# A planner that lands loads in the order of their issue, one load moved behind another, and a new table of due times

## The chip, the cores and the metric

The kernel runs on one core of one Trainium2 chip. The metric is the device time of one execution in microseconds, smaller being better. The time before is a median over three executions. The profile is of one further execution, with its own time.

## The reference: what is computed

Two layers, one after the other. The first is a linear attention with polynomial sketches; B = 4 batches, H = 4 heads, S = 1088 tokens, D = 32, r = 8:

```python
def phi(x):                       # x: (b, h, s, d)
    a = np.einsum('rd,bhsd->bhsr', S1, x)
    b = np.einsum('rd,bhsd->bhsr', S2, x)
    return np.einsum('bhsi,bhsj->bhsij', a, b).reshape(*x.shape[:-1], r * r)
q_p, k_p = (phi(q), phi(k))
kv = np.einsum('bhsf,bhsd->bhfd', k_p, v)
z = np.sum(k_p, axis=2)
num = np.einsum('bhsf,bhfd->bhsd', q_p, kv)
den = np.einsum('bhsf,bhf->bhs', q_p, z)[..., None] + 1e-06
attn = num / den
```

The second is a gated feed-forward layer over the 4352 tokens (B * S) with 128 channels (H * D) and 1536 hidden units: `np.maximum(x @ w_gate, 0) * (x @ w_val) @ w_out`. Inputs and output are float32.

## The kernel before

**Layout and stages.** A batch is 1088 tokens, held as 128 partitions by 34 chunks. For each batch a class K makes the keys' side: two transposes on DVE (kt1, L531), sketches on PE (ksk, L542), transposes back (kt2, L555), the sum z (L570, L584 and the small DVE steps zc and wc), the products of the two sketches on POOL (kphi, L599), the cast of v to 16 bits in two halves (vc, L606, on ACT for batches 1 to 3), the product kv on PE (L613) and its eviction by DVE into bz (kve, L620). A class Q makes the queries' sketches and the denominator (qt1 L1034, qsk L719 or L735, qt2 L741, bw L769, dn L776, rd L781, an L801). A class G makes the query product (qphi, L867), turns it (through PE at L885 and ACT at L892 for the first three groups, through a transposing DMA at L875 for the later ones), multiplies it with bz (num, L901) and writes x, the feed-forward's input, in 16 bits (L908 or L913).

**Feed-forward.** A class F does one unit: gate matmuls g (L960), relu by ACT (L965), value matmuls v (L972), their product h by DVE (L982), and the output matmuls o (L994), which accumulate over the units of a group. In every sixth unit from the fourth on ACT copies the value (vcp, L977) and POOL makes the product instead (hp, L987). There are 103 units: 0 to 23 on batch 0, 24 to 47 on batch 1 and so on, the last seven on the tokens that are left of all batches. At a group's end ACT evicts (L1002) and SP stores (L1011, L1016).

**What sets the order of the work.** Nothing is scheduled at run time. A class Plan holds all operations with an engine, an estimated duration, predecessors, PSUM banks to take and drop, and a due time. `Plan.run` (L89) simulates the engines and starts one operation after the other: it takes the one that can start first (L118), and then, among the operations of the same engine that can start within a short look-ahead, the one with the earliest due time (L120). The order of the starts is the order in which instructions are put into each engine's queue, and each queue is worked off in order. Due times come from the consumers' due times (`dues`, L82), and at the end a hand-held table `shift` (L1107) adds to single operations' due times, in microseconds: negative is earlier.

**Loads.** SP issues all of them on one queue. Up to q1 they stand in program order with fixed times of landing in the plan (`LAND`, L405). The loads after these, v1, k2, q2, v2, k3, q3 and v3, are operations (`load`, L438): one on SP for issuing, one on a further serial engine of the plan, "DMA", for the transfer. Loads of v are four DMAs each (L216), those of k and q one (L210, L273). Buffers of later batches first serve as staging for the feed-forward's weights (L250): k of batch 2 holds two thirds of w_out, v of batch 1 the last third. So k2's load waits for the casts wo0 and wo1, and v1's load for the cast wo2 (POOL, L428); these are the predecessors at L444 and L445. Where two issued transfers stand at the plan's "DMA" engine at once, L120 takes the one that is due earlier, whatever the order of issue.

Of the kernel before, what the change touches and what calls it, by code (L numbers as in the profile page):

```python
# [35 lines left out]
class Plan:  # L36
# [52 lines left out]
    def run(self):  # L89
        todo = [o for o in self.ops if o.start is None]  # L90
        need = {o: sum(a.start is None for a in o.after) for o in todo}
        ready = [o for o in todo if not need[o]]
        n = 0
        while ready:
            for o in ready:
                o.at = max([self.free[o.eng]] + [
                    a.start + a.busy if a.eng == o.eng == "PE" else a.done for a in o.after])
            now = min(o.at for o in ready)

            left = dict(self.banks)  # L100
            wants = sorted((o for o in ready if any(l.banks is None for l in o.take)),
                           key=lambda o: (o.due, o.seq))
            for o in wants:
                near, o.pick, rest = o.at <= now + self.HOLD, [], dict(left)
                for l in o.take:
                    if l.banks is None:
                        got = self.choose(rest, l.n, o.at)
                        if got is None:
                            o.at = None
                            break  # L110
                        o.at = max([o.at] + [rest.pop(b) for b in got])
                        o.pick.append((l, got))
                if near and o.at is not None:
                    left = rest
            can = [o for o in ready if o.at is not None]
            if not can:
                raise RuntimeError("no bank for any of " + ", ".join(o.name for o in ready))
            o = min(can, key=lambda o: (o.at, o.due, o.seq))  # L118

            o = min((c for c in can if c.eng == o.eng and c.at <= o.at + self.look(o)),  # L120
                    key=lambda c: (c.due, c.seq))
            o.start = o.at
            o.done = o.start + o.vis
            self.free[o.eng] = o.start + o.busy
            for l in o.take:
                if l.banks is None:
                    l.banks = next(got for m, got in o.pick if m is l)
                    for b in l.banks:
                        del self.banks[b]
            for l in o.drop:  # L130
                l.left -= 1
                l.free_at = max(l.free_at or 0.0, o.done)
                if not l.left:
                    for b in l.banks:
                        self.banks[b] = l.free_at
            ready.remove(o)
            for s in o.succ:
                need[s] -= 1
                if not need[s]:
                    ready.append(s)  # L140
            n += 1
        assert n == len(todo), [o.name for o in todo if o.start is None]
        return max(o.done for o in todo)
# [3 lines left out]
def kernel(  # L147
# [12 lines left out]
    nc = tc.nc  # L160
# [45 lines left out]
    def flat(src, b):  # L206
        return src[b].rearrange("h (p c) d -> (h p) (c d)", c=NC)

    def load_k(eng, b):
        eng.dma_start(out=k_sb[b][:, 0:NC * D], in_=flat(k, b))  # L210
# [38 lines left out]
    v1, v2 = (v32[b].rearrange("p h c -> p (h c)") for b in (1, 2))  # L249
# [22 lines left out]
    def load_q(eng, b):  # L272
        eng.dma_start(out=q_sb[b], in_=flat(q, b))  # L273

    def load_vs(b):
        for a in (0, 2, 1, 3):
            load_v(nc.sync, b, a)
# [143 lines left out]
    wcast = {}  # L421
# [14 lines left out]
    issue = {}  # L436

    def load(name, fn, after):  # L438
        n = 4 if name[0] == "v" else 1
        issue[name] = i = P.add("SP", f"{name} issue", 0.44 * n, fn, after,  # L440
                                rec=1.95 - 0.44 * n)
        land[name] = P.add("DMA", name, 2.7 if n == 4 else 1.4, None, [i], rec=0.15)

    load("v1", lambda: load_vs(1), [wcast["wo2"]])  # L444
    load("k2", lambda: load_k(nc.sync, 2), [wcast["wo0"], wcast["wo1"]])  # L445
    load("q2", lambda: load_q(nc.sync, 2), [])
    load("v2", lambda: load_vs(2), [wcast["wg2"], wcast["wv2"], land["v1"]])
    load("k3", lambda: load_k(nc.sync, 3), [wcast["wg0"], wcast["wv0"]])
# [587 lines left out]
    qt1 = {}  # L1036
# [64 lines left out]
    for o in P.ops:  # L1101
# [3 lines left out]


    shift = {  # L1107
# [16 lines left out]
    }  # L1124
    for o in P.ops:
        o.due += shift.get(o.name, 0.0)
# [46 lines left out]
```

## Time and profile before

| | |
|---|---|
| median of 3 executions | 100.71 us (99.73 to 101.25) |
| the profiled execution's own time | 101.48 us |
| its span, first to last instruction | 99.70 us |
| granted TensorE clock | 1.00 of full speed |
| busy in the span | PE 93.9, DVE 83.1, ACT 81.0, POOL 61.2 us |
| first feed-forward matmul | 13.77 us |
| DMA | 13.28 MB, mean 133 GB/s |

Rows of the profile name an engine, a line of the kernel, the operation, and the tiles as out<-in. PE is TensorE's matmuls, PEld its weight loads, SPq the issuing of DMAs on SP. A row of the timeline starts with the start and the duration in us, consecutive instructions of one kind merged; in square brackets stands idle time of the engine just before and what ended it.

### The profile page before, as it was taken

To read this page: it belongs to the slowest core of one execution; us is meant where nothing else is said; L and a number is where in the kernel's file an instruction comes from. 1 tells how busy PE (TensorE), PEld (TensorE's weight loads), DVE (VectorE), ACT (ScalarE), POOL (GpSimd) and SP (SyncE) were. 2 spreads that over 40 slices of the span, in tenths; PEclk is the share of its full clock that TensorE was granted. 3 is DMA by queue.
4 is the path that set the end of the run, shared out by engine and by line. 5 is a ranking of instruction groups with operands and counts; after the bars stand their busy time and mean duration, and the time that the engine had idled before them with its cause. 6 is when DMAs were issued, how large, how long until landed. Compare 5 with 4: busy or idle time off the path is not lost.

```text
span 99.7 us, 3026 instructions
## 1 busy us (share of the span) xinstructions
PE 93.9 (94%) x1129; PEld 61.7 (62%) x1129; DVE 83.1 (83%) x181; ACT 81.0 (81%) x160; POOL 61.2 (61%) x66
## 2 busy tenths in 40 slices
PE   6999999999799999999999999999999999999950
PEld 2265678677466665666756765657666565668920
DVE  5979959989799999999999699876869777696940
ACT  3411899978699988989998489899899989999920
POOL 6148569699959699669969944799422404224000
PEclk9999999999999999999999999999999999999999
DMA  2999999786620678950435004015352300210122
GB/s 50 323 250 268 406 410 414 246 274 172 187 78 2 143 136 283 325 151 7 105 85 132 0 7 109 0 29 97 92 117 50 105 7 0 73 33 0 28 57 80
DMA packets 16783, 13.28 MB, mean 133 GB/s; under 512 B 8064, under 2 KB 14464, under 8 KB 16768
## 3 DMA queue, kind: packets, MB, share of 16 engines
q1 hardware_dynamic: 16736, 13.08, 45.3%
q8 instruction: 9, 0.15, 0.7%
q14 instruction: 6, 0.05, 0.2%
q10 hardware_dynamic: 32, 0.00, 0.0%
HBM read 9.14 MB, written 2.23 MB: 114 GB/s over the span
## 4 chain that ended last, share of the span: by engine, by line
PE 67%; DVE 9%; DMA 7%; POOL 5%; SPq 4%; issue 3%; ACT 2%; DVEq 0%; ACTq 0%
PE ps L994 21%; PE ps L960 20%; PE ps L972 19%; DMA q_sb<-in_q_dram 4%; DMA v<-in_v_dram 3%; POOL qqp L867 3%; PE ps L901 3%; SPq L216 3%; PE ps L613 2%; PE ps L735 2%; PE ps L542 1%; ACT g_sb L965 1%; DVE qT L1034 1%; DVE ht L982 1%; POOL wo L428 1%
## 5 line engine op out<-in xcount | busy, mean ns | idle before, releaser
L982 DVE TENSOR_TENSOR ht<-g_sb,ps 128x512 f16<-128x512 f16 (+1 forms) x87 | 55.4, 672 | 10.1 <-ACT g_sb L965 5.2
L965 ACT ACTIVATE g_sb<-ps 128x512 f16<-128x512 f32 (+1 forms) x103 | 56.2, 605 | 5.0 <-PE ps L960 3.7
L960 PE MATMUL ps<-xT,wg 128*128 128x512 f16 (+1 forms) x120 | 37.1, 348 | 0.6 <-ACT g_sb L965 0.6
L972 PE MATMUL ps<-xT,wv 128*128 128x512 f16 (+1 forms) x120 | 37.2, 347 | 0.0
L994 PEld LDWEIGHTS <-ht 128*128 128x128 f16 x408 | 27.6, 98 | 13.5 <-POOL ht L987 3.3
L994 PE MATMUL ps<-wo,ht 128*128 128x128 f16 x408 | 34.7, 219 | 0.2
L987 POOL TENSOR_TENSOR ht<-g_sb,v_sb 128x512 f16<-128x512 f16 x16 | 18.7, 1168 | 18.2 <-ACT g_sb L965 13.5
L599 POOL TENSOR_TENSOR kp<-kab 128x512 f16<-128x512 f32 (+1 forms) x15 | 17.0, 1159 | 2.1 <-DVE kab L555 2.0
L960 PEld LDWEIGHTS <-wg 128*128 128x128 f16 x120 | 13.1, 115 | 5.1 <-issue 1.8
L867 POOL TENSOR_TENSOR qqp<-qan,qabc 128x1024 f16<-128x1024 f32 (+1 forms) x9 | 15.7, 1759 | 0.6 <-DVE qan L801 0.4
L972 PEld LDWEIGHTS <-wv 128*128 128x128 f16 x120 | 12.9, 114 | 4.3 <-issue 0.9
L977 ACT COPY v_sb<-ps 128x512 f32<-128x512 f32 x16 | 9.6, 601 | 0.0
L330 PE MATMUL ps<-zero 128*128 128x512 f16 (+6 forms) x23 | 6.7, 409 | 1.0 <-DVE maskkv L295 1.0
L606 ACT CAST v<-v 128x576 f16<-128x576 f32 x7 | 4.7, 681 | 2.4 <-DMA v<-in_v_dram 2.4
L1002 ACT ACTIVATE o_sb<-ps 128x512 f32<-128x512 f32 (+1 forms) x10 | 5.4, 544 | 1.3 <-PE ps L994 1.2
L1034 DVE STREAM_TRANSPOSE qT<-q_sb 128x576 f32<-128x576 f32 (+4 forms) x10 | 6.1, 614 | 0.5 <-DMA q_sb<-in_q_dram 0.5
L913 ACT CAST xT<-ps 128x512 f16<-128x512 f32 (+1 forms) x9 | 5.0, 554 | 0.7 <-PE ps L901 0.7
L531 DVE STREAM_TRANSPOSE kT<-k_sb 128x544 f32<-128x544 f32 (+2 forms) x8 | 5.5, 719 | 0.0
L901 PE MATMUL ps<-qpt,bz 128*128 128x512 f16 (+2 forms) x26 | 5.3, 305 | 0.0
L741 DVE STREAM_TRANSPOSE qabc<-ps 128x512 f32<-128x512 f32 (+2 forms) x8 | 5.3, 692 | 0.0
L330 PEld LDWEIGHTS <-zero 128*128 128x128 f16 x23 | 2.4, 120 | 3.1 <-issue 1.4
L613 PEld LDWEIGHTS <-kp 128*128 128x128 f16 (+1 forms) x72 | 3.5, 98 | 1.3 <-issue 0.2
(85 smaller groups left out, 64.3 us busy)
## 6 DMA issues: line engine op xcount, KB each, us to landing
v<-in_v_dram SPq DMA_DIRECT2D x15, 144.0 KB, 5.7
out_dram<-o_sb SPq DMA_DIRECT2D x28, 64.0 KB, 1.8
k_sb<-in_k_dram SPq DMA_DIRECT2D x3, 544.0 KB, 5.2
q_sb<-in_q_dram SPq DMA_DIRECT2D x3, 544.0 KB, 7.5
k_sb<-in_moe_w_out_dram SPq DMA_DIRECT2D x2, 256.0 KB, 5.2
q_sb<-in_q_dram SPq DMA_DIRECT2D x1, 416.0 KB, 5.6
k_sb<-in_k_dram SPq DMA_DIRECT2D x1, 288.0 KB, 2.8
k_sb<-in_k_dram SPq DMA_DIRECT2D x1, 256.0 KB, 3.0
```

Of the source, the lines that this page charges most:

```text
L330: nc.tensor.matmul(PS[:, W_BANK, 0:m * w], zero, zero[:, None, 0:w].to_broadcast([128, m, w]), start=True, stop=True)
L599: eng.tensor_tensor(out=self.kp[:, lo:hi].rearrange("p x g (i a c) -> p (x g i) a c", i=2, a=R), in0=src[:, 0, :, :, None].to_broadcast([1 ...
L867: eng.tensor_tensor(out=self.qp[:, lo:hi].rearrange("p x g (i a c) -> p (x g i) a c", i=2, a=R), in0=a_in[:, :, :, None].to_broadcast([128 ...
L901: nc.tensor.matmul(o[:, 0:n * 128].rearrange("f (x t) -> f x t", x=n)[:, :, t], self.ks[b or 0].bz[:, p], self.pt[:, 0:n, p, t], start=(p ...
L960: nc.tensor.matmul(bank(self.lg)[:, y * W:(y + 1) * W], wblock(wg, j), x, start=True, stop=True, skip_group_check=True)
L965: nc.scalar.activation(out=self.gs[:, 0:self.cols], in_=bank(self.lg)[:, 0:self.cols], func=ACTF.Relu)
L972: nc.tensor.matmul(bank(self.lv)[:, y * W:(y + 1) * W], wblock(wv, j), x, start=True, stop=True, skip_group_check=True)
L977: nc.scalar.copy(out=self.vs, in_=bank(self.lv))
L982: nc.vector.tensor_tensor(out=self.ht[:, 0:w], in0=self.gs[:, 0:w], in1=bank(self.lv)[:, 0:w], op=ALU.mult)
L987: nc.gpsimd.tensor_tensor(out=self.ht, in0=self.gs, in1=self.vs, op=ALU.mult)
L994: nc.tensor.matmul(o[:, s], self.ht[:, y * W + s * 128:y * W + (s + 1) * 128], wo[:, j // 4, (j % 4) * DM:(j % 4 + 1) * DM], start=(j == 0 ...
L1034: nc.vector.transpose(qT[b][:, lo * 32:hi * 32], q_sb[b][:, lo * 32:hi * 32])
```

## The change

In `Plan.run` a transfer is chosen by the time its issue started instead of by its due time. The issue of k2 gets v1's issue as a further predecessor, so that it comes after it on SP. The table of shifts is replaced: 74 entries before, 116 after, 47 names in both. The entries on units (g, v, h, o) go from 54 to 89 and reach unit 76 instead of 52. The core of the diff:

```diff
             o = min((c for c in can if c.eng == o.eng and c.at <= o.at + self.look(o)),
-                    key=lambda c: (c.due, c.seq))
+                    key=lambda c: (c.after[-1].start if c.eng == "DMA" else c.due, c.seq))
...
     load("v1", lambda: load_vs(1), [wcast["wo2"]])
-    load("k2", lambda: load_k(nc.sync, 2), [wcast["wo0"], wcast["wo1"]])
+    load("k2", lambda: load_k(nc.sync, 2), [wcast["wo0"], wcast["wo1"], issue["v1"]])
...
     shift = {
...
-        "h 33": -8.2, "h 38": 2.8, "kphi 1 6": -2.9, "ksk 3 0": 0.7,
-        "kt1 3 1": 2.5, "kv 0 4 1": 1.8, "kv 1 0 0": -0.7, "kv 2 0 0": 3.3,
-        "kve 1": 1.1, "num 1,0": 1.7, "num 1,4": 0.8, "o 14": 9.8,
...
-        "qaT 0,0": 5.9, "qsk 2,0": -1.1, "qt1 1 0": 0.2, "qt1 2 16": 4.8,
...
-        "vc 1 0": -1.7, "vc 1 1": -0.2, "w 2": -0.5, "z 3": -2.2,
+        "g 10": -0.4, "g 12": -2.5, "g 16": 0.9, "g 18": 0.4, "g 19": 1.3,
...
+        "h 14": -6.9, "h 24": 0.8, "kphi 2 0": 8.0, "kphi 2 4": 4.9,
+        "ksk 0 1": 4.1, "ksk 3 0": 0.7, "kt1 3 0": -4.6, "kt1 3 1": 2.1,
+        "kv 0 8 0": 2.0, "kv 1 6 0": 1.3, "kv 2 0 0": 3.9, "kve 1": 3.1,
+        "num 1,0": 1.7, "num 1,4": 1.6, "num 2,4": -2.2, "num 3,0": 0.9,
...
+        "o 70": 1.9, "o 8": 5.1, "qphi 0,0 0": 5.1, "qsk 0,0 0": 5.6,
+        "qt1 3 0": -1.6, "qt1 3 16": -1.0, "qt2 2,0 1": 2.3, "qt2 3,0 0": 5.4,
+        "rd 3,0": -0.6, "sx": -2.9, "v 0": -1.5, "v 11": -0.5, "v 12": -1.1,
...
+        "z 2": -0.2, "zc 0": -3.2,
     }
```

27 rows, old and new, of the table shift are left out of this document.

## The prediction

> **What bounds the kernel now.** I read the page first, then the PE groups kept apart by shape, the busy time by stages, and last the order of work on SP, ACT, POOL, DVE and PE around the one stage that is not full. The page's busy times, with their share of the span:
>
> ```profile
> PE 93.9 (94%) x1129; PEld 61.7 (62%) x1129; DVE 83.1 (83%) x181; ACT 81.0 (81%) x160; POOL 61.2 (61%) x66
> ```
>
> A busy PE need not be PE at its peak, so I take the spacing of its matmuls from the chain of waits (start, us, what) and the counts from the groups by shape (count | busy, mean ns):
>
> ```profile
> 43.88 0.89 PE ps L994 x16
> 44.78 0.43 PE ps L960 x2
> ...
> 92.91 0.22 PE ps L960 x2
> ```
> ```profile
> L994 PE MATMUL ps<-wo,ht 128*128 128x128 f16 x408 | 34.7, 219 | 0.2
> L972 PE MATMUL ps<-xT,wv 128*128 128x512 f16 x84 | 30.7, 379 | 0.0
> L960 PE MATMUL ps<-xT,wg 128*128 128x512 f16 x84 | 30.6, 380 | 0.6 <-ACT g_sb L965 0.6
> L960 PE MATMUL ps<-xT,wg 128*128 128x256 f16 x36 | 6.8, 274 | 0.0
> ```
>
> The last group has its twin of 36 on the v side (L972). Spacing is 0.43/2 = 0.215 us at 512 columns, 0.22/2 = 0.11 at 256, 0.89/16 = 0.056 at 128. The feed-forward stream is therefore 168 x 0.215 + 72 x 0.11 + 408 x 0.056 = 36.1 + 7.9 + 22.8 = 66.8 us of PE, and the attention matmuls lie between them. The stages (window; its length; then PE, PEld, DVE, ACT, POOL busy) show where that stream stands still:
>
> ```profile
> 25.00:30.00 5.00, 4.40 (x49) 2.84 (x48) 4.20 (x8) 4.32 (x9) 3.71 (x5) 1.00 0.49 131
> 30.00:35.00 5.00, 5.00 (x66) 3.11 (x62) 5.00 (x10) 4.94 (x10) 4.14 (x4) 1.00 0.31 73
> ...
> 80.00:90.00 10.00, 10.00 (x99) 6.56 (x97) 7.56 (x12) 9.46 (x20) 2.33 (x2) 1.00 0.11 28
> 90.00:99.70 9.70, 6.01 (x70) 4.94 (x67) 5.17 (x9) 5.37 (x12) 1.17 (x1) 1.00 0.15 42
> ```
>
> From 30 on PE is covered to the last stage, at a granted clock of 1.00. The only hole is in 25 to 30. The order on ACT, then on PE, names it and gives its size (start, us; in brackets the idle time before and what ended it):
>
> ```profile
> 25.68 0.68 ACT L606 CAST v<-v 128x576 f16<-128x576 f32 x1 [0.78 <-DMA v<-in_v_dram]
> ...
> 35.38 0.59 ACT L913 CAST xT<-ps 128x512 f16<-128x512 f32 x1 [0.30 <-PE ps L901]
> ```
> ```profile
> 25.92 0.38 PE L972 MATMUL ps<-xT,wv 128*128 128x512 f16 x1
> 26.90 0.38 PE L960 MATMUL ps<-xT,wg 128*128 128x512 f16 x1 [0.60 <-ACT g_sb L965]
> ...
> 36.04 0.39 PE L994 MATMUL ps<-wo,ht 128*128 128x128 f16 x4
> 36.27 0.38 PE L960 MATMUL ps<-xT,wg 128*128 128x512 f16 x1
> ```
>
> ACT stands in its queue at the cast of batch 1's v (vc 1 0), which has not landed; the relu behind it frees no bank, and PE starts nothing between 25.92 and 26.90. Of those 0.98 us the matmul's own spacing is 0.215, so PE lost 0.76 us. The cast waits for v because of what SP did (start, us of issuing):
>
> ```profile
> 18.18 0.33 SPq L210 DMA_DIRECT2D k_sb<-in_k_dram  x1
> 18.74 3.30 SPq L216 DMA_DIRECT2D v<-in_v_dram  x4
> 22.32 2.28 SPq L1011 DMA_DIRECT2D out_dram<-o_sb  x4
> 24.65 1.85 SPq L216 DMA_DIRECT2D v<-in_v_dram  x4
> ```
>
> The last v issue of batch 1 only goes out at about 21.6. Batch 2's four (the last row) need 1.85 us instead of 3.30.
>
> **The change part by part.** *SP's order.* k2's issue leaves its place ahead of v1's four and goes behind them. No DMA is added or removed, and none is issued by POOL. v1 cannot go before 18.74, because it overwrites the buffer that the third wo cast reads, and that cast ends there:
>
> ```profile
> 18.10 0.62 POOL L428 CAST wo<-v 128x512 f16<-128x512 f32 x1
> ...
> 26.02 1.17 POOL L987 TENSOR_TENSOR ht<-g_sb,v_sb 128x512 f16<-128x512 f16 x1
> 28.40 0.63 POOL L801 TENSOR_TENSOR qan<-qabc,qrd 128x256 f32<-128x256 f32 x1 [1.21 <-DVE qrd L781]
> 29.11 1.96 POOL L867 TENSOR_TENSOR qqp<-qan,qabc 128x1024 f16<-128x1024 f32 x1
> ```
>
> So v1's four issues start at 18.7 as before, but with no 544 KB load just ahead of them. At v2's 1.85 us they end at 20.6. For the landings I take batch 2's v as the nearest row (issues, KB each, median us to landing; the window of v2, then that of k2):
>
> ```profile
> v<-in_v_dram SPq DMA_DIRECT2D x4, 144.0 KB, 2.8
> ```
> ```profile
> k_sb<-in_k_dram SPq DMA_DIRECT2D x1, 544.0 KB, 6.1
> ```
>
> The fourth issue at 18.74 + 1.85 x 3/4 = 20.1 plus 2.8 gives 22.9 for v1; an upper bound is k2's own 6.1 us after 18.74, 24.8. Both end before ACT came free at 25.68 - 0.78 = 24.90, so the 0.78 us wait goes in either case, and with it PE's 0.76. What waits at SP behind v1's wait for the cast is k2 (0.56 us from 18.18 to 18.74) and, much later, the first stores at 22.32, which SP reaches free.
>
> *k2 later.* It is issued at about 20.6 instead of 18.18, and lands at 20.6 + 6.1 = 26.7 instead of 24.3. Its reader is the transpose of batch 2's keys:
>
> ```profile
> 30.23 1.36 DVE L531 STREAM_TRANSPOSE kT<-k_sb 128x544 f32<-128x544 f32 x2
> ...
> 33.29 0.28 DVE L620 TENSOR_TENSOR bz<-ps,maskkv 128x128 f16<-128x128 f32 x1
> ```
>
> Cost 0, covered by 30.23 - 26.7 = 3.5 us. If the new order put that transpose over 3.5 us earlier, DVE would stand, up to 1.36 us of its work late.
>
> *The planner's tie rule.* It issues nothing itself. It decides where the planner believes a load has landed, hence where vc 1 0 stands on ACT. With v1 issued first, belief and queue agree. Lower bound 0, upper bound the 0.76 already counted; I count it once.
>
> *Batch 1's chain.* The gain at 26 only reaches the end if batch 1's first x comes earlier as well, since PE runs out of batch 0's units at about 36.0 and takes the next g at 36.27, right after x (ACT 35.38 to 35.97). In the POOL rows qan waited 1.21 us for DVE's reciprocal, which stood behind an h that waited for the same relu. With the stall gone qan starts when hp ends, 27.19, and x can come 1.2 us earlier against the 0.76 that PE needs. So the 0.76 passes through.
>
> *Shifts of the start* ("qsk 0,0 0", "qphi 0,0 0", "ksk 0 1", "sx", "zc 0" added, "qaT 0,0" gone). No row shows the new order. DVE before the first x:
>
> ```profile
> 10.10 0.75 DVE L867 TENSOR_TENSOR qqp<-ps,qabc 128x256 f16<-128x256 f32 x2
> 10.76 0.19 DVE L781 RECIPROCAL qrd<-qdn 128x8 f32<-128x8 f32 x1
> ```
>
> If the reciprocal goes ahead of both products, x can gain up to 0.66 us (10.76 - 10.10); if the deferred product comes out last, x can lose as much. I take 0, as DVE is covered there and the same work has to pass; both ends go into the range.
>
> *Shifts of the units and the later batches* (89 entries on g, v, h and o instead of 54, kve 1 deferred by 2.0 more, two kphi 2 deferred). They move no work off PE and PE has no hole after 30. Cost 0 by PE's cover. The best that is left is the tail's wait of PE's weight loads for DVE, the worst is a late x at a change of batch (a rival below).
>
> ```profile
> PEld L994 <- DVE ht L982: 0.5, 2, 0.3
> ```
>
> **The sum.** The profiled execution took 101.48 us, its span 99.70 (the end of the last stage), so 1.78 lies around it. 101.48 - 0.76 = 100.72 by its own time. It stood 0.77 above the median of the runs, 100.71; there the same sum gives 99.95, so I predict 99.9.
>
> Two rules against it. The spacing of 0.215 us above makes PE the bound. The Trainium skill, "TensorE: Matmul & The Clock Gate", Back-to-back issue gap, gives about 131 ns as the sustained spacing at 512 columns; then PE would have slack and the time would follow batch 1's chain, which is the rival "PE is not the bound" below. This case's rows, 0.43 for two, speak against that figure. The order of landing in the rows is k2 at 18.18 + 6.1 = 24.3, then v1. The Trainium skill, "DMA: Bandwidth & Descriptors", Queues, rings and completion order, says that completion is not first-in first-out for one issuing engine; if v1 did not pass k2 the sum would be 0 and the time 100.7. The rows show the order kept.
>
> **The rivals.** *PE is not the bound.* The time follows batch 1's chain and gains POOL's 1.21: 100.71 - 1.21 = 99.5. For it: 94% busy counts pipelined matmuls. Against it: full cover from 30 to 90.
>
> *The wait goes and nothing is gained.* v1 is not earlier, or the 0.76 is given back at 36 because x of batch 1 is held by something else, kve 1 above all, which ran at 33.29 and is deferred by 2.0 us more. Time 100.7.
>
> *Everything fits.* Stall 0.76, start 0.66 and tail 0.5 are all saved: 100.71 - 1.92 = 98.8, and with the runs' spread some of it under 98.7. Against it: the start and the tail need luck in orders that no row shows.
>
> *The handover slips (slower).* PE has nothing but batch 1's units after 36.0. If POOL takes other ready work ahead of batch 1's query product, say an hp (1.17) and the second product (1.96, as the first), x comes 3.1 us later and PE stands for it: 100.71 - 0.76 + 3.1 = 103.0. It decides once x is later than about 36; 2% are reached at a slip of 2.8. For it: POOL works from 26.02 to 31.07 with one wait of 1.21, so any job put ahead there delays x, and 42 more due times are shifted than before. Against it: query products have early due times.
>
> **How the numbers follow.** Forecast 0.44, PE not the bound 0.06, nothing gained 0.13, everything fits 0.13, handover slips 0.24. Low 98.6 is "everything fits" less 0.2 for the spread of the runs, 99.73 to 101.25 (0.08 lies under it), high 103.0 is the slip (some 0.11 lies over it). The forecast's own range, with the start at either end, is 99.3 to 100.6. 2% is about what a measurement of this kernel can tell from no change: faster by more (under 98.7) 0.13, within 0.63, slower (over 102.7) 0.24.
>
> **What would show it.** Right: SP issues v1's four at 18.7 in under 2 us and k2 after them; ACT's cast of batch 1's v has no wait for the DMA; PE has no hole near 26; the first g of batch 1 is earlier than 36.27 by about 0.8. Wrong: PE idle at 34 to 38 or at a later change of batch, DVE waiting for k2, or a first g of the whole kernel later than before. The prediction fails in size if the span's end moves by other than the holes in PE's stream.

## The result, and the profile after

| | before | changed |
|---|---|---|
| median of 20 executions | 101.24 us | 99.97 us |
| from to | 99.73 to 104.20 us | 99.24 to 103.88 us |
| ratio, with its 95% interval | | 0.9936 (0.9909 to 0.9963) |

The ratio compares undisturbed executions only, which is why it is nearer to 1 than that of the two medians. It is a gain of 0.0064 x 101.24 = 0.65 us (0.37 to 0.92). The prediction had 100.71 - 0.76 = 99.95, a ratio of 0.992. The 0.76 lies inside the interval of the measured gain. That the median of 99.97 stands so near to 99.95 is in part chance: over 20 executions the kernel before has a median of 101.24 instead of 100.71, and from there the same 0.76 would give 100.48. The prediction took 2% for about the least that can be told from no change; over 20 executions each, 0.6% can.

Two profiled executions of the changed kernel matter here. The first took 101.42 us (span 99.6), no less than the 101.48 of before. The second, e3, took 99.82 us (span 98.0). The first one's rows say why (timeline of ACT, then of PE: start, us; in brackets the idle time before and what ended it):

```profile
15.32 0.62 ACT L427 CAST wg<-v 128x512 f16<-128x512 f32 x1 [1.30 <-DMA v<-in_moe_w_gate_dram]
```
```profile
15.23 0.38 PE L973 MATMUL ps<-xT,wv 128*128 128x256 f16 x2
16.49 0.38 PE L886 MATMUL ps<-ident,qqp 128*128 128x128 f16 x4 [0.88 <-ACT g_sb L966]
```

A load of gate weights, which the change does not touch, landed late; ACT stood at its cast, and PE stood 16.49 - 15.23 - 2 x 0.11 = 1.04 us. The loads of the start land at different times from one execution to the next, with either kernel. So I read the change from e3 and use the first profile only beside it.

The rows of e3 that answer to those of before: the page's busy times, the issues on SP, the landings in that window, ACT, and the stage of the hole (window; its length; busy time of PE, PEld, DVE, ACT, POOL).

```profile
PE 93.8 (96%) x1130; PEld 62.0 (63%) x1130; DVE 83.2 (85%) x181; ACT 81.6 (83%) x160; POOL 61.3 (62%) x66
```
```profile
18.66 2.53 SPq L217 DMA_DIRECT2D v<-in_v_dram  x4
21.23 0.43 SPq L211 DMA_DIRECT2D k_sb<-in_k_dram  x1
```
```profile
v<-in_v_dram SPq DMA_DIRECT2D x4, 144.0 KB, 3.0
```
```profile
24.70 0.69 ACT L607 CAST v<-v 128x576 f16<-128x576 f32 x1
```
```profile
25.00:30.00 5.00, 5.00 (x58) 3.38 (x57) 4.97 (x10) 5.00 (x11) 4.46 (x5) 1.00 0.45 128
```

The busy times are the same work in a shorter span. Batch 1's v goes out first, its cast has no bracket (no wait), and PE's 4.40 of 5.00 us in 25 to 30 has become 5.00, with 58 matmuls in place of 49. But the span is 99.70 - 98.0 = 1.7 us shorter than that of the profile of before, where the prediction had 0.76, and PE had, by the busy times, nothing else to gain. Where most of the rest lies, the gate matmuls show, which are the same 120 in both kernels: the starts of the first, the 37th (first of batch 1), the 61st, the 85th and the last cut the span into stages. Rows of before (that of the 37th, 36.27, stands in the prediction), then of e3:

```profile
13.77 0.60 PE L960 MATMUL ps<-xT,wg 128*128 128x256 f16 x4
...
55.65 0.38 PE L960 MATMUL ps<-xT,wg 128*128 128x512 f16 x1
...
74.01 0.38 PE L960 MATMUL ps<-xT,wg 128*128 128x512 f16 x1
...
94.29 0.27 PE L960 MATMUL ps<-xT,wg 128*128 128x256 f16 x1
```
```profile
13.68 0.38 PE L961 MATMUL ps<-xT,wg 128*128 128x256 f16 x2
...
35.29 0.59 PE L961 MATMUL ps<-xT,wg 128*128 128x512 f16 x2
...
54.52 0.38 PE L961 MATMUL ps<-xT,wg 128*128 128x512 f16 x1
...
72.23 0.59 PE L961 MATMUL ps<-xT,wg 128*128 128x512 f16 x2
...
93.05 0.27 PE L961 MATMUL ps<-xT,wg 128*128 128x256 f16 x1
```

The table gives the differences of such starts for every profiled execution. Matmuls other than g move over the cuts when the order changes, so between two orders only the sum of the last three columns of stages counts.

| profiled execution | first g at | to batch 1 | batch 1 | batch 2 | batch 3 to last g | sum of the last three |
|---|---|---|---|---|---|---|
| before | 13.77 | 22.50 | 19.38 | 18.36 | 20.28 | 58.02 |
| before again (e5, e9, e10) | 14.56, 13.79, 13.52 | 21.85, 22.03, 22.51 | 19.38 | 18.38 to 18.39 | 20.27 to 20.28 | 58.03 to 58.05 |
| changed, first | 14.14 | 22.75 | 19.22 | 17.71 | 20.82 | 57.76 |
| changed, e3 | 13.68 | 21.61 | 19.22 | 17.71 | 20.82 | 57.75 |
| e1, k2's place alone | 13.81 | 21.61 | 19.38 | 18.36 | 20.27 | 58.01 |
| e2, the table alone | 14.30 | 22.26 | 19.22 | 17.71 | 20.82 | 57.75 |
| e4, two casts later | 13.16 | 22.64 | 19.38 | 18.36 | 20.28 | 58.02 |
| e6, casts and kv later | 16.43 | 22.28 | 19.39 | 18.38 | 20.27 | 58.04 |
| e7, a load more ahead of v | 13.64 | 25.98 | 19.38 | 18.35 | 20.27 | 58.01 |
| e8, k2's place and three o's | 13.64 | 21.74 | 19.38 | 18.15 | 20.19 | 57.72 |
| e11, the load behind v | 13.76 | 21.61 | 19.38 | 18.34 | 20.29 | 58.01 |
| e12, changed and one o | 13.68 | 21.62 | 19.22 | 17.71 | 20.73 | 57.66 |

From the last g to PE's end it is 1.91 to 1.93 us in all of them. After the first stage, executions of one order agree within 0.06 us in a stage and within 0.04 in the sum of the three. The new order gains 58.02 - 57.75 = 0.27 us there, which the prediction had at 0. The first stage gains 22.50 - 21.61 = 0.89 against the profile of before, but the four executions of before differ in it by 0.66 us. The first g is 0.09 earlier. The last 0.42 us lies behind PE's end: from there to the end of the span it is 3.50 us in the profile of before (3.51 in e7), 3.08 in e3 and 3.07 to 3.16 in all others. Before, SP spent 2.22 us on issuing the last store but one (94.70 to 96.92), so the last store began at 97.02, though ACT's last eviction (0.39 us from 96.24) had ended 0.4 us earlier; in e3 the store began at 95.42, right behind the eviction (0.38 us from 95.00). The other three executions of before have 3.09 to 3.15 as well, so this part is one execution's and not the change's.

### The profile page after: what moved, and what is told of

It reads as the page before. It is cut to its first block, busy times and chain, and to the rows that moved or that the text cites. A ratio compares the mean times of both kernels' runs of the same rounds, so it can differ in the third digit from the quotient of the medians.

```text
span 99.6 us, 3006 instructions
## 1 busy us (share of the span) xinstructions
PE 93.6 (94%) x1130; PEld 62.0 (62%) x1130; DVE 83.4 (84%) x181; ACT 81.5 (82%) x160; POOL 61.1 (61%) x66
## 4 chain that ended last, share of the span: by engine, by line
PE 79%; DMA 12%; SPq 2%; issue 1%; ACT 1%; DVE 1%; ACTq 0%; DVEq 0%
PE ps L995 23%; PE ps L961 22%; PE ps L973 21%; DMA v<-in_v_dram 6%; DMA v<-in_moe_w_gate_dram 6%; PE ps L902 4%; PE ps L736 2%; PE ps L543 2%; PE ps L614 2%; PE ps L571 1%; PE ps L886 1%; DVE ht L983 1%; ACT g_sb L966 1%; PE ps L585 1%; SPq L235 0%
## 5 line engine op out<-in xcount | busy, mean ns | idle before, releaser
L961 PE MATMUL ps<-xT,wg 128*128 128x512 f16 (+1 forms) x120 | 36.5, 349 | 0.0
L973 PE MATMUL ps<-xT,wv 128*128 128x512 f16 (+1 forms) x120 | 35.7, 347 | 0.0
L995 PEld LDWEIGHTS <-ht 128*128 128x128 f16 x408 | 26.6, 98 | 11.1 <-DVE ht L983 2.6
L995 PE MATMUL ps<-wo,ht 128*128 128x128 f16 x408 | 32.6, 219 | 0.2
L331 PE MATMUL ps<-zero 128*128 128x512 f16 (+5 forms) x24 | 6.9, 420 | 1.0 <-DVE maskkv L296 1.0
```

Of the source, the lines that this page charges most:

```text
L331: nc.tensor.matmul(PS[:, W_BANK, 0:m * w], zero, zero[:, None, 0:w].to_broadcast([128, m, w]), start=True, stop=True)
L961: nc.tensor.matmul(bank(self.lg)[:, y * W:(y + 1) * W], wblock(wg, j), x, start=True, stop=True, skip_group_check=True)
L973: nc.tensor.matmul(bank(self.lv)[:, y * W:(y + 1) * W], wblock(wv, j), x, start=True, stop=True, skip_group_check=True)
L995: nc.tensor.matmul(o[:, s], self.ht[:, y * W + s * 128:y * W + (s + 1) * 128], wo[:, j // 4, (j % 4) * DM:(j % 4 + 1) * DM], start=(j == 0 ...
```

## The experiments

The theory was that v1 behind k2 makes ACT stand at the cast of batch 1's v, that PE stands for it, and that every such microsecond of PE is one of the time. The rivals: the gain comes from the new due times and not from the load; or it is ACT's queue alone that matters, and casts placed later would do as well; or PE is not the bound.

**k2's place alone (e1).** Only the added predecessor; on all engines but SP the order of instructions is that of before. The rule for ties has nothing to decide here: with k2 behind v1, the plan's orders are the same with the rule and without it.

```diff
-    load("k2", lambda: load_k(nc.sync, 2), [wcast["wo0"], wcast["wo1"]])
+    load("k2", lambda: load_k(nc.sync, 2), [wcast["wo0"], wcast["wo1"], issue["v1"]])
```

> The kernel before, with k2's issue put behind v1's four on SP and nothing else moved on any engine. Theory 1 (the load's place in SP's queue): v of batch 1 lands about 2 us earlier, ACT's first cast of it has no wait, PE's hole of 0.76 us near 26 is gone, ratio to before 0.992 to 0.994, so all of the measured gain. Rival 1 (the new due times bring the gain): ratio 0.998 to 1.002. Rival 2 (the hole goes and is given back at the change to batch 1): no hole at 26, a new one near 36, ratio 0.998 to 1.002.

Measured: 100.41 us against 100.88, ratio 0.9964 (0.9932 to 0.9996): a gain, but smaller than the 0.992 to 0.994 expected, so part of the whole and not all of it. The timeline of PE in e1 around 26, then the transpose of batch 2's keys on DVE, then PE at the change of batch:

```profile
25.96 0.38 PE L972 MATMUL ps<-xT,wv 128*128 128x512 f16 x1
26.18 0.38 PE L960 MATMUL ps<-xT,wg 128*128 128x512 f16 x1
...
26.61 0.28 PE L613 MATMUL ps<-v,kp 128*128 128x64 f16 x4
26.73 0.38 PE L960 MATMUL ps<-xT,wg 128*128 128x512 f16 x1
```
```profile
29.38 1.36 DVE L531 STREAM_TRANSPOSE kT<-k_sb 128x544 f32<-128x544 f32 x2
```
```profile
35.42 0.38 PE L960 MATMUL ps<-xT,wg 128*128 128x512 f16 x1
```

The spacing of v and g is 0.22 again: no hole. The later k2 is waited for by nobody, and the gain passes the change of batch. In before the four kv matmuls, which take 0.12 here, took 0.22 (timeline of PE):

```profile
27.33 0.38 PE L613 MATMUL ps<-v,kp 128*128 128x64 f16 x4
27.55 0.39 PE L960 MATMUL ps<-xT,wg 128*128 128x512 f16 x1
```

That is a second, small hole of 0.10 us, at the place where the second half of the cast ended (26.75 + 0.66 = 27.41 on ACT). The prediction did not have it; with the 0.76 it accounts for nearly all of the 0.89.

**The table alone (e2).** k2 stays ahead of v1 on SP; all other queues have the changed kernel's order.

```diff
-        "dn 3,0": 3.7, "g 0": -0.6, "g 10": -0.5, "g 11": 0.6, "g 12": -4.3,
...
+        "g 10": -0.4, "g 12": -2.5, "g 16": 0.9, "g 18": 0.4, "g 19": 1.3,
...
```

> The kernel before with the new table of due times alone; the order on all engines but SP is that of the changed kernel, on SP k2 is still ahead of v1. Theory 1: ACT waits again at the cast of batch 1's v and PE has a hole of 0.5 to 0.8 us near 26, ratio 0.999 to 1.002. Rival 1: no hole that matters, ratio about 0.994.

Measured: 100.48 us, ratio 0.9943 (0.9911 to 0.9976). The stall is still there; the timeline of ACT:

```profile
25.98 0.67 ACT L606 CAST v<-v 128x576 f16<-128x576 f32 x1 [0.49 <-DMA v<-in_v_dram]
```

and the sum of the late stages is 57.75, as in the changed kernel. So the table brings a gain of its own, about 0.26 us of PE's time after 36. The ratio was expected at 0.999 to 1.002 and came out near the 0.994 of the rival: it is 0.57 us (0.24 to 0.90), and the traces' 0.26 lies at the edge of that interval. Whether the table gains more than the one profile of e2 shows stays open, and by the times alone it cannot be said whether k2's place or the table gains more.

**The changed kernel again (e3).**

> The changed kernel once more, for a profile beside the others. All theories: ratio 0.991 to 0.996. In its profile I expect no wait of ACT for batch 1's v, no hole in PE near 26, and the wait for the feed-forward's weights near 15 that the first profile of it showed to be smaller or absent, since its loads came later from the start in that execution.

Measured: 100.08 us, ratio 0.9917 (0.9883 to 0.9951), which overlaps the interval over the 20 executions. Its profile is the one shown above; near 15, where PE stood 1.04 us in the first profile, it stands 0.11 us.

**The casts later, k2 still ahead (e4).** The order that ACT and PE get is changed by hand, the loads stay.

```diff
+    for n, t in (("vc 1 0", 25.80), ("vc 1 1", 26.28), ("kv 1 0 0", 26.30)):
+        next(o for o in P.ops if o.name == n).start = t
```

> The kernel before with its SP order (k2 ahead of v1), but with the two casts of batch 1's v put one place and one and a half later on ACT, behind relus that were ready (and the first kv matmuls behind them on PE). Theory 1 in its narrower form, that the hole is made by the cast standing ahead of ready relus in ACT's queue: the wait goes to 0.2 us or less and PE's hole with it, ratio 0.992 to 0.995 with no load moved. Rival 3 (batch 1's chain needs v earlier, ACT's order is no matter): the hole moves, ratio 0.998 to 1.002.

Measured: 101.35 us, ratio 1.0056 (1.0023 to 1.0089): slower, where a gain was expected. ACT, then PE:

```profile
25.74 0.67 ACT L606 CAST v<-v 128x576 f16<-128x576 f32 x1
```
```profile
26.49 0.19 PE L613 MATMUL ps<-v,kp 128*128 128x64 f16 x1
27.52 0.36 PE L613 MATMUL ps<-v,kp 128*128 128x64 f16 x7 [0.84 <-ACT v L606]
```

ACT no longer waits for the load, but PE's kv now stands for the cast, 27.52 - 26.49 = 1.03 us with one matmul in it. The theory that ACT's queue alone matters falls in this form: the reader of the cast has to move as well.

**Casts and kv later (e6).** As e4, with the kv matmuls 1.7 us later still.

```diff
+    for n, t in (("vc 1 0", 25.8), ("vc 1 1", 26.28), ("kv 1 0 0", 28.02), ("kv 1 2 0", 28.03), ("kv 1 4 0", 28.04)):
+        next(o for o in P.ops if o.name == n and o.fn).start = t
```

> The kernel before with k2 ahead of v1 on SP as it was, the two casts of batch 1's v later on ACT, and the first three kv matmul groups of batch 1 later on PE, behind two g and one o. Theory 1 with what the last set showed (two in-order queues stand in turn, ACT at the cast and PE at kv): no hole over 0.25 us between 25 and 28, from the first g to the last 0.5 to 0.9 us less than before, ratio 0.992 to 0.997. Rival 3 (batch 1's chain itself needs v earlier): a hole near 35, at the change to batch 1, ratio 0.998 or more.

Measured: 100.88 us, ratio 1.0004 (0.9968 to 1.0039): no gain. Its profiled execution is a poor guide: it took 103.53 us, its granted clock was 0.50 from 10 to 14, and its first g came some 3 us late, with v1's issue as late (21.40 on SP). The cast does not wait for v there, but another hole is seen, at a g that waits for the relu behind the moved casts:

```profile
29.97 0.83 PE L994 MATMUL ps<-wo,ht 128*128 128x128 f16 x12
31.29 0.59 PE L960 MATMUL ps<-xT,wg 128*128 128x512 f16 x2 [0.48 <-ACT g_sb L965]
```

Of the 1.32 us between them twelve o matmuls take 0.67, so 0.65 is lost, it seems to the edit itself. The experiment is inconclusive: it cannot say whether some later place for casts and kv would do what the moved load does.

**Before, profiled again (e5, e9, e10).** No edit. The question was how much of the 0.76 is that one execution.

> The kernel before once more, for a second profile. The first profile has SP's four issues of batch 1's v at 3.30 us and PE's hole at 0.77; two other kernels with k2 ahead showed 1.75 us for the four. Theory 1: the hole follows the landing of v, so with issues of 1.75 us it is 0.3 to 0.7 us here; the small holes at an o that waits for a product of POOL (0.2 near 62, 0.15 near 79) are there again.

> The kernel before once more, for a third profile. The two so far differ in one place alone, PE's hole near 26 (0.77 and 0.13 us). Theory 3 (the hole is the time by which v of batch 1 lands after ACT reaches its cast, and both vary from execution to execution): ACT's wait for the DMA and PE's hole are both between 0 and 0.8 us and equal within 0.2; the stages from the first g of batch 1 on are 19.38, 18.36 and 20.27 us again, within 0.03.

> As the run before, a fourth profile of the kernel before: a hole between 0 and 0.8 us that goes with ACT's wait, the later stages the same within 0.03 us.

Measured: 101.32, 100.69 and 100.85 us. SP and PE of e5, then of e10:

```profile
19.53 1.75 SPq L216 DMA_DIRECT2D v<-in_v_dram  x4
```
```profile
26.72 0.38 PE L972 MATMUL ps<-xT,wv 128*128 128x512 f16 x1
27.06 0.38 PE L960 MATMUL ps<-xT,wg 128*128 128x512 f16 x1
```
```profile
18.49 2.59 SPq L216 DMA_DIRECT2D v<-in_v_dram  x4
```
```profile
25.67 0.38 PE L972 MATMUL ps<-xT,wv 128*128 128x512 f16 x1
26.67 0.38 PE L960 MATMUL ps<-xT,wg 128*128 128x512 f16 x1 [0.62 <-ACT g_sb L965]
```

Less the spacing of 0.215, the hole is 0.13 us in e5, 0.79 in e10, 0.29 in e9 and was 0.76 in the profile of the prediction: a mean of 0.49. The stage up to batch 1, which holds the second hole too, is 22.22 us in the mean of the four, 0.61 over e1's 21.61. The 0.13 of e5 is under the 0.3 to 0.7 expected for it. In all four, ACT came free for the cast 6.16 us after v1's first issue, while the cast began 6.31, 6.96, 6.47 and 6.94 us after it (order as above: e5, e10, e9, first profile); so the landing alone makes the difference. SP's four issues took 1.75, 2.59, 1.75 and 3.30 us in the same order, and k2's load, which was issued just ahead of them, took 5.3, 6.1, 5.3 and 6.1 us to land: where both took long, the hole is large. Which of the two drives the other, the traces do not show. The gain of k2's place is therefore 0.24 to 0.90 us by the execution, 0.61 in the mean; e1's ratio is 0.36 us with an interval of 0.04 to 0.69, which holds the mean of 0.61 but not the 0.76 of the prediction.

**A load more, ahead of v1 (e7).** 544 KB that nobody reads, issued between k2 and v1.

```diff
+    pad = sb([128, NC * D], FP32, "pad")
+
+    def load_k2():
+        load_k(nc.sync, 2)
+        nc.sync.dma_start(out=pad, in_=flat(k, 3))
...
-    load("k2", lambda: load_k(nc.sync, 2), [wcast["wo0"], wcast["wo1"]])
+    load("k2", load_k2, [wcast["wo0"], wcast["wo1"]])
```

> The kernel before with one more load of 544 KB, into a tile that nobody reads, between k2's issue and v1's four on SP; nothing else is moved. Theory 1: v lands 1.2 to 1.8 us later, ACT's wait and PE's hole grow by as much, ratio 1.010 to 1.018. Rival 1 (the place in the queue matters little): under 1.004.

Measured: 103.96 us, ratio 1.0266 (1.0196 to 1.0336), more than expected. Landings, ACT and PE:

```profile
v<-in_v_dram SPq DMA_DIRECT2D x4, 144.0 KB, 7.1
```
```profile
27.48 0.67 ACT L612 CAST v<-v 128x576 f16<-128x576 f32 x1 [2.71 <-DMA v<-in_v_dram]
```
```profile
25.79 0.38 PE L978 MATMUL ps<-xT,wv 128*128 128x512 f16 x1
28.70 0.38 PE L966 MATMUL ps<-xT,wg 128*128 128x512 f16 x1 [2.52 <-ACT g_sb L971]
```

PE stands 28.70 - 25.79 - 0.215 = 2.69 us for ACT's 2.71. That is 2.2 more than the 0.49 that the four executions of before have in the mean. But the stage up to batch 1 is 25.98, 3.8 over their mean of 22.22, so 1.5 us more are lost behind the hole. Two windows of e7 (length; busy time of PE, PEld, DVE, ACT, POOL; granted clock; DMA) and PE's timeline there say where:

```profile
29.00:30.00 1.00, 1.00 (x13) 0.62 (x12) 0.97 (x3) 1.00 (x3) 0.00 (x0) 0.99 0.75 187
30.00:31.00 1.00, 1.00 (x14) 0.76 (x10) 0.89 (x3) 1.00 (x3) 0.72 (x2) 0.50 0.12 30
```
```profile
31.73 1.06 PE L966 MATMUL ps<-xT,wg 128*128 128x512 f16 x2
32.58 0.63 PE L978 MATMUL ps<-xT,wv 128*128 128x512 f16 x1
```

Some 1.3 us after PE went on, its granted clock was 0.50 and stayed there to about 33.2; two matmuls of 512 columns took 0.85 instead of 0.43. The stages after that are unchanged. The six executions of e7 agree with this, as far as the hole of the one profiled stands for all: two with a mean clock of 1.00 took 102.68 and 103.19 us, 2.3 over the mean of before on that chip (100.64), which is the 2.2 us of hole, one for one; four with 0.977 to 0.979 took 103.78 to 104.83, some 3.6 over it. Of the 79 executions of before that ran beside the experiments, one has a mean clock under 0.99 (0.983). The theories had priced the hole alone; the clock is what the expectation lacked. The Trainium skill, "TensorE: Matmul & The Clock Gate", Part 1: The HAM clock gate, has the clock fall to half after an idle window of about 3.4 us, with windows that run free of the kernel. The half agrees with the 0.50 of the rows; but 2.69 us of standing were enough here, and in e6's profiled execution the clock was 0.50 from 10 to 14 with no idle time of PE over 1.0 us ahead of it in the span. So a long hole is not the only occasion for the fall; that the hole of e7 brings it is argued from the row's place and from the four executions of six. That four executions show the fall and two do not would suit a free-running window, which no run here tests.

**The same load behind v1 (e11).** v1, then the extra load, then k2.

```diff
+    pad = sb([128, NC * D], FP32, "pad")
+
+    def load_k2():
+        nc.sync.dma_start(out=pad, in_=flat(k, 3))
+        load_k(nc.sync, 2)
...
+    load("k2", load_k2, [wcast["wo0"], wcast["wo1"], issue["v1"]])
```

> The kernel before with v1's four issues ahead of k2, and the same extra load of 544 KB as in the earlier run, now behind v1 and ahead of k2. Theory 1 (the place in the queue decides, not the bytes): no wait of ACT for v, no hole near 26, ratio 0.994 to 0.999, against 1.027 with the same load ahead of v1. Rival 5 (the bytes on the DMA engines are what costs): a hole of over 1 us at 26 or later, ratio over 1.005.

Measured: 100.54 us against 100.65, ratio 1.0012 (0.9974 to 1.0051). Landings and ACT:

```profile
v<-in_v_dram SPq DMA_DIRECT2D x4, 144.0 KB, 3.4
```
```profile
24.77 0.69 ACT L612 CAST v<-v 128x576 f16<-128x576 f32 x1
```

No wait, and its stages are e1's. The same bytes make a hole of 2.69 us ahead of v and none behind it. Its ratio lies a little over the expected one; the interval overlaps e1's, but what the load may cost elsewhere (up to about 0.5 us) stays open, since its one profiled execution, with a span of 98.4 like e1's, does not show it.

**k2's place and three o's (e8).** The due times of before, but three of its output matmuls a few places later. I chose those three because PE stood there in before, as the timeline of PE, then of its weight loads shows for the first of them:

```profile
61.88 0.59 PE L901 MATMUL ps<-qpt,bz 128*128 128x512 f16 x2
62.52 0.62 PE L994 MATMUL ps<-wo,ht 128*128 128x128 f16 x8
```
```profile
62.52 0.34 PEld L994 LDWEIGHTS <-ht 128*128 128x128 f16 x6 [0.54 <-POOL ht L987]
```

Two matmuls of 512 columns take 0.43, so the o could start at 62.31 and starts at 62.52: it waits 0.2 us for a product h that POOL makes. The busy time of the stages counts this as full, because a record of 0.38 us outlasts the 0.215 to the next matmul:

```profile
27.00:94.00 67.00, 66.96 (x776) 44.02 (x776) 58.28 (x101) 62.06 (x122) 41.65 (x35) 1.00 0.32 82
```

```diff
+    for n, t in (("o 52", 61.0), ("o 76", 77.86), ("o 82", 82.27)):
+        next(o for o in P.ops if o.name == n and o.fn).start = t
```

> The kernel before with k2 behind v1 on SP, and three output groups whose products POOL makes (o 52, o 76, o 82) one place later on PE; the old due times. Theory 2 (what the new due times bring is that the o of a POOL unit is no longer put ahead of work that is ready): the holes near 61, 78 and 83 are under 0.06 us, from the first g to the last 0.3 to 0.45 us less than with k2 behind v1 alone (79.62), ratio 0.990 to 0.994, as the changed kernel or better. Rival 4 (the gain of the due times comes from the start or from many small places): no more than 0.1 us less, ratio as with k2 behind v1 alone, 0.996.

Measured: 99.99 us, ratio 0.9931 (0.9896 to 0.9966). The o 52 in e8, with the two matmuls ahead of it, follows at 0.43:

```profile
61.00 0.59 PE L901 MATMUL ps<-qpt,bz 128*128 128x512 f16 x2
61.43 0.61 PE L994 MATMUL ps<-wo,ht 128*128 128x128 f16 x8
```

The sum of the late stages is 57.72, 0.29 under e1's. Three moved o's bring as much as the whole new table brings there (0.26), and the time is that of the changed kernel. Two parts of the expectation were missed: near 78 a hole of 0.12 us is left, now ahead of num (L901), and from the first g to the last it is 79.46 us, 0.16 less than e1's 79.62 instead of 0.3 to 0.45, because the first stage was 0.13 longer in this execution, before any of the moved o's.

**The changed kernel with o 82 later (e12).** One such hole is left in the changed kernel (timeline of PE in e3), 0.35 - 0.215 = 0.13 us:

```profile
82.29 0.38 PE L961 MATMUL ps<-xT,wg 128*128 128x512 f16 x1
82.64 0.62 PE L995 MATMUL ps<-wo,ht 128*128 128x128 f16 x8
```

```diff
+    for n, t in (("o 82", 82.17),):
+        next(o for o in P.ops if o.name == n and o.fn).start = t
```

> The changed kernel with one output group whose product POOL makes (o 82) put behind the next one on PE. Theory 2: the hole of 0.14 us near 82 goes, the rest stays as in the changed kernel's second profile; ratio to before 0.001 to 0.002 below the changed kernel's 0.992 to 0.994, which the interval cannot show but the profile can: 20.82 becomes 20.65 to 20.72 us in the last stage.

Measured: 99.82 us, ratio 0.9916 (0.9878 to 0.9953). The last stage is 20.73 instead of 20.82, close to the 20.65 to 20.72 expected. That is the fastest version here, but 0.09 us is under what the times can tell, so only the trace shows it.

## Why the prediction was right, and which step failed

*The stall and its cause* were right. With v1 ahead, its landing takes 3.0 us instead of 5.6, ACT's wait and PE's hole at 26 are gone (e1, e3), a further load ahead makes both larger (e7), and the same load behind does not (e11).

*Its size* was off. The term of 0.76 us was read from a single execution, where SP's issues took 3.30 us. Over four executions the hole is 0.49 in the mean, and 0.61 with what goes along with it: 0.15 us too much by the traces. By e1's times it is 0.36 us, and 0.76 lies above their whole interval.

*The step that failed* is "PE has no hole after 30. Cost 0 by PE's cover". The shifts gain 0.26 us after batch 1's start (e2, e3). Covered 66.96 of 67.00 us, PE still lost 0.2 us at a time at o's that waited for POOL's h. I had taken the spacing of matmuls for the feed-forward's sum and then went back to busy time for the cover; the same spacing, 0.43 for two, would have shown 62.52 - 61.88 as 0.64. The waits of PE's weight loads for POOL named it too, between 13 and 94 (us in total, times, longest), first before, then in e3:

```profile
PEld L994 <- POOL ht L987: 3.3, 10, 0.5
```
```profile
PEld L995 <- POOL ht L988: 2.1, 7, 0.5
```

And it is there that the new table gains. By start to start, PE stands 0.21, 0.15 and 0.08 us before at the o's near 62, 79 and 84 that wait for POOL; in e3 the first two holes are gone and the third is 0.14. That is 0.30 less, against 0.27 by the stages.

The two errors, 0.15 too much and 0.26 too little, partly cancel: 0.61 + 0.26 = 0.87 us by the traces, 0.76 forecast, 0.65 (0.37 to 0.92) measured. The closeness of 99.95 and 99.97 owes something to that, and to the median of three executions from which the sum started.

*k2 later at no cost* was right: the transposes run at 29.38 in e1 without a wait, after k2's issue at 21.30. *Four issues in under 2 us* was not quite: 2.48 in e1, 2.53 in e3, 1.75 in the first profile after. *The tie rule* moved nothing with k2 behind v1. *The gain passes through batch 1's chain*: the first g of batch 1 is at 35.42 and 35.29 instead of 36.27 (36.14 in the mean of the four executions of before), about the 0.8 that was asked for, and no hole came at 36, so kve 1's deferral did no harm and the slower rival, the slip at the handover, did not happen. *The start's shifts* at 0: the first g came at 13.52 to 14.56 in four executions of before and at 13.68 to 14.30 with the new table (e2, e3, e12 and the first); any effect is smaller than that spread, and was not resolved. *The tail* of PE did not move (1.91 to 1.93 us from the last g). The span's end did move by more than the holes in PE's stream, which the prediction gave as a sign of failing in size: 0.42 us of it is SP's late last store in the first profile.

*PE is not the bound*, the rival by the shorter spacing, falls: what PE stands longer passes into the time one for one as long as the clock stays (e7, two executions, if their hole was the profiled one's), and two matmuls of 512 columns are 0.43 us apart in e8 as before. The Trainium skill, "TensorE: Matmul & The Clock Gate", Back-to-back issue gap, gives 131 ns; no run here shows it. On landing, v came 7.1 us after its issue behind two loads of 544 KB (e7), 5.0 to 5.7 behind one (the four executions of before) and 3.0 behind none (e1, e3). The Trainium skill, "DMA: Bandwidth & Descriptors", Queues, rings and completion order, says that completion need not be first-in first-out; for these loads the order was kept as far as the wait shows.

The range of 98.6 to 103.0 was wide for what happened; its slow side, 2.3% over 100.71, was the slip at the handover, and its fast side also asked for gains at the start and the tail that no run showed.

## What to carry to other kernels

When an engine is the bound, read its cover from the spacing of starts and not from busy time: a pipelined matmul's record outlasts its slot, and holes of 0.1 to 0.2 us vanish in a stage that is busy to 100%. A stall on a load that has only just not landed varies from execution to execution, so look at several profiles before its length becomes a term of a sum. And where loads share a queue, put the one with the earliest reader first, even when its buffer comes free a little later: the load that moves back costs nothing as long as its reader has slack.

## What the runs showed of the hardware that was not expected

SP's issue of the same four loads took 1.75, 1.75, 2.59 and 3.30 us in four executions of the kernel before, with the same instructions ahead of it; k2's load took 5.3, 5.3, 6.1 and 6.1 us to land in them, and nothing in the traces says why. The issue of one store took 2.22 us in the first profile, against 0.43 in e3. The first feed-forward matmul came at 13.16 to 14.56 us, on loads whose issue the edits do not touch (16.43 in e6's profiled execution, at a granted clock of 0.50 from 10 to 14), while each stage after batch 1's start repeats to 0.06 us for one order. And in e7's profile a hole of 2.69 us on PE was followed by a granted clock of 0.50 for some 3 us, which cost 1.5 us beyond the hole; four of six executions have the mean clock that goes with it.
